# Sliding-window attention and an MLP: q and k loaded two tokens to a partition, turned and multiplied in 64x64 tiles

## The chip, the cores and the metric

The kernel runs on one core of a Trainium2 chip. The metric is device time in microseconds (us) for one execution, and a kernel's time is the median of its runs. Engine names are those of the profile: PE is the matrix engine (a matmul streams a moving operand against a stationary one that a weight load, PEld in the profile, put there before), DVE the vector engine, ACT the scalar engine (activations), POOL the engine whose queue issues the loads here, SP the queue that issues the stores. Matmul results land in PSUM, which has eight banks of 2 KB per partition; everything else lies in SBUF.

## What is computed

Eight batches, eight heads, 576 tokens, head size 64, model width 512, hidden width 2048. Attention looks back over a window of 128 tokens with a linear distance penalty per head; its output goes through a normalised MLP with a residual. Inputs and output are float32; the kernel computes in fp16 with float32 sums.

```python
def _attn_ref(q, k, v):                      # B, H, S, D = 8, 8, 576, 64
    scores = np.matmul(q, k.transpose(0, 1, 3, 2)) / np.sqrt(D)
    rel = pos[:, None] - pos[None, :]
    slopes = 2.0 ** (-8.0 * (np.arange(H) + 1) / H)
    mask = (rel >= 0) & (rel < 128)
    scores = np.where(mask, scores - slopes * np.abs(rel), -1e9)
    attn = softmax(scores)
    return np.matmul(attn, v)

def _moe_ref(x, g_ln, w_ch1, w_ch2):         # x: [B, S, H * D]
    xn = (x - mean) / np.sqrt(var + 1e-06) * g_ln
    return x + np.maximum(xn @ w_ch1, 0.0) @ w_ch2
```

## The kernel before

**Blocks.** Two batches make a pair (four pairs). A pair has nine blocks of 128 tokens: four of the even batch, four of the odd one, and a ninth (`T`) that holds the last 64 tokens of both. `order` lists the 36 blocks. A block passes through these steps:

- `load_t` (L177) and `load_v` (L185) bring q, k and v by POOL's queue, one token to a partition, all eight heads beside each other; the float32 is turned into fp16 on the way. In HBM one head of one token is a run of 64 numbers.
- `turn` (L228) transposes q and k by PE, eight 128x128 transposes a block (two heads, 64 rows each, in one), into a PSUM tile `ps_tr`. DVE copies the halves of q into `qT` (L232), which holds each head's q in its own half of the rows with zeros in the other half (`zero_rows`, L160 and L161, writes the zeros); ACT copies k into `kT` (L236).
- `scores` (L260) multiplies, by key block and pair of heads, 128 keys with the 256 queries that can see them. Because of the zeros in `qT` one matmul of 128 rows gives two heads beside each other, 512 columns. ACT takes the exponential (L261), DVE multiplies it with the mask and distance penalty (`m_full` and its three relatives, L266).
- `values` (L282) multiplies the weights with v, which has a column of ones beside it, so that the row sums come along; DVE takes the reciprocal (L290) and scales (L291).
- `centre` takes mean and variance (L316, L317) and subtracts the mean (L319); `turn_x` (L329) transposes the result by PE and DVE copies it to `xT` (L330). `inv_std` computes 1/std on DVE for a group of blocks.

**Groups.** `GROUPS` has sizes 2, 2 and then eight times 4. For a group `mlp` does the first product (L407, 16 units of four matmuls, each followed by a ReLU on ACT, L414) and the second (L419, 16 matmuls a block, then DVE adds the residual at L429 and SP stores).

**Order.** `steps` is a list of closures for the attention part. The MLP of group g is written out unit by unit, and after each unit `advance_to` runs as many steps for later groups as keep both in proportion. In what order each engine then takes its instructions is decided by a scheduler, by readiness and the order of writing.

**Start.** The loads are one list, issued by `load_until` three blocks ahead (`AHEAD`); the weights stand in it behind blocks 1, 2 and 3 (`weights`), w1 in four chunks and w2 in four. `gain_w1` (L149) multiplies w1 with the gain on DVE, all four chunks after block 1.

**PSUM.** Two banks for scores, one for transposes, two for values, three for the MLP.

Of the kernel before, what the change touches and what calls it, by code (L numbers as in the profile page):

```python
# [1 line left out]

# [14 lines left out]
P = 128  # L17
# [4 lines left out]
E0, O0, T = 0, 4, 8  # L22
NSLOT = 9


SLOT = [4, 5, 6, 7, 0, 1, 2, 3, 8]
DURING = {0: [2], 1: [3], 2: [T], 3: [4, 5], 4: [6], 5: [7], 6: [9], 7: [10], T: []}
GROUPS = [2, 2] + [4] * 8

NV = 14  # L30
AHEAD = 3
LEAD = 4

# [4 lines left out]
def distances():  # L38

    key = np.arange(P)[:, None]

    def far(rel, ok):
        return np.where(ok & (rel >= 0) & (rel < WINDOW), rel, FAR)

    q = np.arange(2 * P)[None, :]
    full = far(q - key, np.ones((P, 2 * P), bool))
    tail = np.arange(P)[None, :]  # L50
    even = far(P + tail - key, tail + 0 * key < 64)
    odd = far(P + tail - 64 - key, tail + 0 * key >= 64)
    both = far(tail - key, (tail // 64) == (key // 64))
    return np.concatenate([full, even, odd, both], axis=1).astype(np.float16)
# [3 lines left out]
def kernel(  # L58
# [19 lines left out]
    half = P // 2  # L78
    inv_sqrt_d = float(1.0 / np.sqrt(D))

    def pool(name, bufs, **kw):
# [3 lines left out]
    qk_pool = pool("qkstage", 4)  # L85
    k_pool = pool("kT", 4)
    probs_pool = pool("probs", 7)
# [6 lines left out]
    ps_tr = pool("ps_tr", 1, space=PSUM)  # L94
    ps_pv = pool("ps_pv", 2, space=PSUM)
# [9 lines left out]
    m_full = consts.tile([P, H, 2 * P], FP16)  # L105
    m_even, m_odd, m_both = (
        consts.tile([P, H, P], FP16, name=f"m{i}", tag=f"m{i}") for i in range(3)
    )

    def decay(m, at):  # L110
# [15 lines left out]

    qT = [
        consts.tile([P, HP, 2, NSLOT, P], FP16, name=f"qT{i}", tag=f"qT{i}")  # L130
        for i in range(2)
    ]
# [26 lines left out]
    def zero_rows(i):  # L159
        nc.vector.memset(qT[i][half:P, :, 0, :, :], 0.0)  # L160
        nc.vector.memset(qT[i][0:half, :, 1, :, :], 0.0)  # L161


    def spans(p, blk):

        if blk == T:
            return [(2 * p, 4 * P, TAIL, 0), (2 * p + 1, 4 * P, TAIL, half)]
        b, i = (2 * p, blk) if blk < O0 else (2 * p + 1, blk - O0)
        return [(b, i * P, P, 0)]

    staged = {}

    def load_t(src, tag, p, blk):
        st = qk_pool.tile([P, H, D], FP16, tag=tag, name=tag)
        staged[tag, p, blk] = st
        for b, t0, n, p0 in spans(p, blk):
            nc.gpsimd.dma_start(  # L177
                out=st[p0 : p0 + n, :, :],
                in_=src[b, :, t0 : t0 + n, :].rearrange("h p d -> p h d"),
            )  # L180
# [11 lines left out]
    turns = [(0, [E0, E0 + 1])]  # L192
    for p, blk in order:
        turns.append((p, DURING[blk]))
    turns = [
        [(p + (i >= NSLOT), i % NSLOT) for i in l if p + (i >= NSLOT) < NPAIR]
        for p, l in turns
    ]
    w1s, w2s = ([(f, c) for c in range(4)] for f in (load_w1, load_w2))
    weights = {1: w1s[:2], 2: w1s[2:], 3: w2s}  # L200
    loads, place = [], []
    for n, (p, blk) in enumerate(order):
        for t in turns[n]:
            loads += [(load_t, q, "qs") + t, (load_t, k, "ks") + t]
        place.append(len(loads))
        loads.append((load_v, p, blk))
        loads += weights.get(n, [])
# [10 lines left out]
    probs, xs = {}, {}  # L218

    kT = {}  # L220

    def turn(p, blk, pool=ps_tr, tag="tr"):

        qs, ks = staged.pop(("qs", p, blk)), staged.pop(("ks", p, blk))
        ps = pool.tile([P, 2 * HP, P], FP16, tag=tag, name="ps_tr")
        for i, st in enumerate((qs, ks)):
            for hp in range(HP):
                nc.tensor.transpose(  # L228
                    ps[:, i * HP + hp, :], st[:, 2 * hp : 2 * hp + 2, :], iden
                )  # L230
        for i, rows in enumerate((slice(0, half), slice(half, P))):
            nc.vector.tensor_copy(  # L232
                out=qT[p % 2][rows, :, i, SLOT[blk], :], in_=ps[rows, 0:HP, :]
            )
        kT[p, blk] = k_pool.tile([P, HP, P], FP16, tag="kT", name="kT")
        nc.scalar.copy(out=kT[p, blk], in_=ps[:, HP:, :])  # L236

    def scores(p, blk, hp):


        if hp == 0:
            w = P if blk == T else 2 * P
            probs[p, blk] = probs_pool.tile([P, H, w], FP16, tag="probs", name="probs")
        pr = probs[p, blk]
        qt = qT[p % 2][:, hp]
        heads = slice(2 * hp, 2 * hp + 2)
        own, nxt = slice(0, P), slice(P, 2 * P)
        at = SLOT[blk]
        if blk == T:
            nq, rhs = 1, qt[:, :, at, :]  # L250
            weigh = [(own, m_both[:, heads, :])]
        elif blk % 4 == 3:
            nq, rhs = 2, qt[:, :, at : SLOT[T] + 1 : SLOT[T] - at, :]
            m_next = m_even if blk == E0 + 3 else m_odd
            weigh = [(own, m_full[:, heads, own]), (nxt, m_next[:, heads, :])]
        else:
            nq, rhs = 2, qt[:, :, at : at + 2, :]
            weigh = [(slice(0, 2 * P), m_full[:, heads, :])]
# [226 lines left out]
```

## Time and profile before

The median of three runs is 363.92 us (363.85 to 365.21). The profiled execution took 363.87 us; its span, from the first to the last instruction, is 362.1 us.

| | busy, us | share of the span | instructions |
|---|---|---|---|
| PE, matmuls | 337.1 | 93% | 2336 |
| PEld, weight loads | 174.0 | 48% | 2336 |
| DVE | 237.1 | 65% | 717 |
| ACT | 185.1 | 51% | 373 |
| POOL | 107.0 | 30% | 132 |

| group (line) | count | busy, us | mean ns of one |
|---|---|---|---|
| first MLP product (L407) | 640 | 144.5 | 359 |
| second MLP product (L419) | 576 | 141.2 | 379 |
| scores (L260) | 144 | 52.9 | 385 |
| values (L282) | 544 | 32.3 | 196 |
| transposes of q (L228) | 144 | 14.9 | 230 |
| mask products on DVE (L266), 128x512 of m_full | 96 | 40.5 | 423 |
| qT copies on DVE (L232) | 72 | 30.3 | 420 |
| kT copies on ACT (L236) | 36 | 20.9 | 584 |

An instruction's mean is its whole way through the engine. Matmuls follow each other more closely than that, since the next one enters while the last one drains; the pace, from start to start, is read from a timeline. A busy PE is therefore not yet a PE at its pace. The chain of work that ended last is 67% PE by time, 17% DVE and 8% ACT.

### The profile page before, as it was taken

The numbers are of one execution on the slowest core, as the hardware profiler recorded it, in microseconds if no ns is written. First come the engines' busy times: TensorE is split into PE (matmuls) and PEld (weight loads), VectorE is DVE, ScalarE is ACT, GpSimd is POOL, SyncE is SP. The second block draws the span as 40 slices with busy tenths as digits, with TensorE's granted clock in tenths as the row PEclk, the third lists the DMA queues.
The fourth block names the chain that finished last, engine by engine and source line by source line (L and its number), as shares of the span: only waits on it lengthen the run. The fifth ranks groups of instructions, "written<-read, shape, count | busy, mean of one in ns | idle before, by whom it ended". The sixth has DMA issues, their size and how long they took to land.

```text
span 362.1 us, 6199 instructions
## 1 busy us (share of the span) xinstructions
PE 337.1 (93%) x2336; PEld 174.0 (48%) x2336; DVE 237.1 (65%) x717; ACT 185.1 (51%) x373; POOL 107.0 (30%) x132
## 2 busy tenths in 40 slices
PE   2369999999999999999999999999999999999994
PEld 1136657554445454544555455554545454454441
DVE  5399899975677567856775678667765775564011
ACT  8526558457426753564357634743576347513700
POOL 8646688631224224223224213112110000000000
PEclk9999999999999999999999999999999999999998
DMA  9999999988689748829689765508640120011012
GB/s 106 171 186 206 159 172 156 100 99 53 42 105 111 51 32 101 103 16 72 87 103 64 52 83 90 35 2 102 89 29 2 58 60 1 2 58 58 2 58 59
DMA packets 122830, 28.39 MB, mean 78 GB/s; under 512 B 113968, under 2 KB 118192, under 8 KB 122800
## 3 DMA queue, kind: packets, MB, share of 16 engines
q0 software_dynamic: 116736, 18.36, 70.7%
q1 hardware_dynamic: 6064, 9.64, 7.8%
q8 instruction: 18, 0.29, 0.3%
q14 instruction: 12, 0.10, 0.1%
HBM read 36.90 MB, written 9.44 MB: 128 GB/s over the span
## 4 chain that ended last, share of the span: by engine, by line
PE 67%; DVE 17%; ACT 8%; DMA 3%; POOL 2%; issue 2%; ACTq 0%; POOLq 0%
PE ps_m L419 27%; PE ps_m L407 24%; PE ps_sc L260 5%; PE ps_pv L282 4%; PE ps_tr L228 3%; ACT probs L261 3%; PE ps_tx L329 3%; DVE probs L266 3%; ACT ht L414 3%; DMA w<-in_moe_w_ch_dram 3%; DVE x L291 3%; DVE st L316 2%; DVE qT L232 2%; DVE o L429 2%; ACT kT L236 2%
## 5 line engine op out<-in xcount | busy, mean ns | idle before, releaser
L407 PE MATMUL ps_m<-xT,w 128*128 128x512 f16 (+1 forms) x640 | 144.5, 359 | 0.0
L419 PE MATMUL ps_m<-w,ht 128*128 128x512 f16 x576 | 141.2, 379 | 0.0
L261 ACT ACTIVATE probs<-ps_sc 128x512 f16<-128x512 f32 (+1 forms) x144 | 80.9, 578 | 89.0 <-PE ps_sc L260 88.7
L414 ACT ACTIVATE ht<-ps_m 128x512 f16<-128x512 f32 (+1 forms) x160 | 89.0, 560 | 43.2 <-PE ps_m L407 42.2
L407 PEld LDWEIGHTS <-w 128*128 128x128 f16 x640 | 59.7, 98 | 50.4 <-issue 0.9
L419 PEld LDWEIGHTS <-ht 128*128 128x128 f16 x576 | 53.4, 98 | 54.3 <-issue 1.6
L266 DVE TENSOR_TENSOR probs<-probs,m_full 128x512 f16<-128x512 f16 (+1 forms) x128 | 49.7, 389 | 44.7 <-ACT probs L261 42.8
L177 POOL DMA_DIRECT2D qs<-in_q_dram x40 | 34.1, 852 | 101.0 <-PE ps_tr L228 85.5
L260 PE MATMUL ps_sc<-qT,kT 128*128 128x512 f16 (+1 forms) x144 | 52.9, 385 | 2.5 <-ACT probs L261 1.3
L185 POOL DMA_DIRECT2D vx<-in_v_dram x40 | 33.9, 860 | 52.6 <-PE ps_pv L282 49.4
L429 DVE SCALAR_TENSOR_TENSOR o<-ps_m,rstd,x 128x512 f32<-128x512 f32 x36 | 26.9, 746 | 25.4 <-PE ps_m L419 24.9
L282 PEld LDWEIGHTS <-probs 128*128 128x128 f16 x544 | 27.1, 98 | 26.7 <-DVE probs L266 12.7
L282 PE MATMUL ps_pv<-vx,probs 128*128 128x65 f16 x544 | 32.3, 196 | 6.9 <-DVE probs L266 6.6
L232 DVE COPY qT<-ps_tr 64x512 f16<-64x512 f16 x72 | 30.3, 420 | 9.1 <-PE ps_tr L228 8.6
L177 POOL DMA_DIRECT2D ks<-in_k_dram x40 | 34.1, 855 | 4.0 <-DMA w<-in_moe_w_ch_dram 2.1
L236 ACT COPY kT<-ps_tr 128x512 f16<-128x512 f16 x36 | 20.9, 584 | 24.9 <-DVE qT L232 23.3
L291 DVE TENSOR_TENSOR x<-ps_pv,rec 128x256 f16<-128x256 f32 x72 | 30.2, 423 | 1.9
L316 DVE BATCH_NORM_STATS2 st<-x 128x6 f32<-128x512 f16 x36 | 25.0, 693 | 1.0
L330 DVE COPY xT<-ps_tx 128x512 f16<-128x512 f16 x36 | 15.2, 424 | 11.8 <-PE ps_tx L329 11.6
L228 PE MATMUL ps_tr<-iden,qs 128*128 128x128 f16 x144 | 14.9, 230 | 7.5 <-DMA qs<-in_q_dram 6.5
L260 PEld LDWEIGHTS <-kT 128*128 128x128 f16 x144 | 14.2, 100 | 14.9 <-issue 2.0
L228 PEld LDWEIGHTS <-qs 128*128 128x128 f16 x144 | 11.4, 102 | 16.6 <-DMA qs<-in_q_dram 7.0
(29 smaller groups left out, 143.7 us busy)
## 6 DMA issues: line engine op xcount, KB each, us to landing
out_dram<-o SPq DMA_DIRECT2D x32, 256.0 KB, 2.6
qs<-in_q_dram POOLq DMA_DIRECT2D x32, 128.0 KB, 4.1
ks<-in_k_dram POOLq DMA_DIRECT2D x32, 128.0 KB, 4.9
vx<-in_v_dram POOLq DMA_DIRECT2D x32, 128.0 KB, 5.3
w<-in_moe_w_ch_dram POOLq DMA_DIRECT2D x8, 512.0 KB, 9.9
out_dram<-o SPq DMA_DIRECT2D x8, 128.0 KB, 2.8
qs<-in_q_dram POOLq DMA_DIRECT2D x8, 64.0 KB, 4.3
ks<-in_k_dram POOLq DMA_DIRECT2D x8, 64.0 KB, 4.0
```

Source lines behind the costliest of these rows:

```text
L177: nc.gpsimd.dma_start(out=st[p0 : p0 + n, :, :], in_=src[b, :, t0 : t0 + n, :].rearrange("h p d -> p h d"),)
L228: nc.tensor.transpose(ps[:, i * HP + hp, :], st[:, 2 * hp : 2 * hp + 2, :], iden)
L232: nc.vector.tensor_copy(out=qT[p % 2][rows, :, i, SLOT[blk], :], in_=ps[rows, 0:HP, :])
L260: nc.tensor.matmul(ps, kT[p, blk][:, hp, :], rhs, start=True, stop=True)
L261: nc.scalar.activation(out=pr[:, heads, :], in_=ps, func=AF.Exp, scale=inv_sqrt_d)
L266: nc.vector.tensor_tensor(out=dst, in0=dst, in1=mask, op=ALU.mult)
L282: nc.tensor.matmul(ps[:, i, :], probs[p, o][:, h, cols], vext[(p * NSLOT + o) % NV][:, h, :], start=(n == 0), stop=(n == len(terms) - 1),)
L291: nc.vector.tensor_tensor(out=xs[p, blk][:, hg * 4 * D : (hg + 1) * 4 * D].rearrange("p (h d) -> p h d", h=4), in0=ps[:, :, 0:D], in1=rec. ...
L407: nc.tensor.matmul(ps[:, 0:cols], w1[:, kb, fb * P : (fb + 1) * P], xT[:, kb, 0:cols], start=(kb == 0), stop=(kb == NKB - 1),)
L414: nc.scalar.activation(out=ht[:, fb, 0:cols], in_=ps[:, 0:cols], func=AF.Relu)
L419: nc.tensor.matmul(ps, ht[:, fb, at * P : (at + 1) * P], w2[:, fb, :], start=(fb == 0), stop=(fb == NFB - 1),)
L429: nc.vector.scalar_tensor_tensor(out=o, in0=ps, scalar=rs[:, at : at + 1], in1=xs[p, blk], op0=ALU.mult, op1=ALU.add,)
```

## The change

- **Loads.** `load_qk` replaces `load_t`: a partition gets two neighbouring tokens, so one head of a partition is a run of 128 numbers in HBM. A tile holds the same 128 tokens of both batches of a pair, 64 partitions each. The number of loads of q, k and v stays 40 each.
- **Block order.** Blocks alternate between the two batches (`divmod(blk, 2)`), the loads of q and k come every second block.
- **Turning.** `turn` (new L215) does two blocks at once in 64x64 tiles: 64 transposes for q and k, each with its own weight load of 64 columns, four in a row on four different quarters of the array. q is copied by DVE and k by ACT, one copy for both blocks (L224); q goes to ACT for the first two turns. `qT` and its zeros are gone.
- **Scores.** By query block instead of key block (`attend`, new L253): 64x64 tiles, the two heads of a pair in the two row halves, the keys in two column halves, 128 queries as columns. A burst of 16 pairs of weight load and matmul fills a PSUM tile of two banks; an ordinary block has two bursts, the block `T` three, the first block of each batch one. One exponential and one mask product of 128x1024 follow each burst.
- **PSUM.** Four banks for scores and the turns of q and k together (two buffers of two banks), one for values and `turn_x` together, three for the MLP.
- **Order of PE.** `manual_schedule` keeps PE's instructions in the order of writing; for the first stage DVE's too.
- **Start.** Groups are 2, 2, 2, 2 and then seven times 4. All weights stand behind the loads of the first four blocks. The first products of groups 0 and 1 come before the second product of group 0; gains for the last three chunks of w1 are spread over the first product of group 0. Two masks' worth of tables (`m_ends`, `m_tail`) replace three.

```diff
-GROUPS = [2, 2] + [4] * 8
-
-NV = 14
-AHEAD = 3
-LEAD = 4
+GROUPS = [2] * 4 + [4] * 7
+
+NV = 10
+AHEAD = 4
+LEAD = 3
...
-    ps_tr = pool("ps_tr", 1, space=PSUM)
-    ps_pv = pool("ps_pv", 2, space=PSUM)
+    ps_pv = pool("ps_pv", 1, space=PSUM)
...
+    def load_qk(src, tag, p, i):
+
+        n = min(P, S - i * P)
+        t = raw_pool.tile([P, H, 2, D], FP16, tag=tag, name=tag)
+        raw[tag, p, i] = t
+        for b in range(2):
             nc.gpsimd.dma_start(
-                out=st[p0 : p0 + n, :, :],
-                in_=src[b, :, t0 : t0 + n, :].rearrange("h p d -> p h d"),
+                out=t[b * n // 2 : (b + 1) * n // 2],
+                in_=src[2 * p + b, :, i * P : i * P + n, :].rearrange(
+                    "h (c r) d -> c h r d", r=2
+                ),
             )
...
-    weights = {1: w1s[:2], 2: w1s[2:], 3: w2s}
+    weights = {3: w1s + w2s}
...
+    def turn(p, i):
...
+        ps = ps_sc.tile([P, 2, 2, 2, HP, HALF], FP16, tag="sc", name="ps_tr")
+        nb = 1 if i == 4 else 2
+        for n, tag in enumerate("qk"):
+            st = raw.pop((tag, p, i))
             for hp in range(HP):
...
+                for r in range(2):
+                    for b in range(nb):
+                        rows = slice(b * HALF, (b + 1) * HALF)
+                        for j in range(2):
+                            cols = slice(j * HALF, (j + 1) * HALF)
+                            nc.tensor.transpose(
+                                ps[cols, b, n, r, hp, :],
+                                st[rows, 2 * hp + j, r, :],
+                                iden[rows, rows],
+                            )
...
+    def attend(p, blk, keys, mask, tag, hps):
...
+        ps = ps_sc.tile([P, 2, len(hps), nk, P], FP32, tag="sc", name="ps_sc")
+        qt, b = turned["q", p, blk // 2], blk % 2
+        for n, hp in enumerate(hps):
+            for t, o in enumerate(keys):
+                kt = turned["k", p, o // 2][:, o % 2]
+                for j in range(2):
+                    rows = slice(j * HALF, (j + 1) * HALF)
+                    for c in range(2):
+                        cols = slice(c * HALF, (c + 1) * HALF)
+                        nc.tensor.matmul(
+                            ps[cols, j, n, t, :],
+                            kt[rows, hp, cols],
+                            qt[rows, b, hp, :],
+                            start=True,
+                            stop=True,
+                        )
...
+    def scores(p, blk):
+        low, high, every = [0, 1], [2, 3], [0, 1, 2, 3]
         if blk == T:
...
+            attend(p, T, [6, 7], m_ends, "probs", low)
+            attend(p, T, [6, 7], m_ends, "probs", high)
+            attend(p, T, [T], m_tail, "own", every)
+        elif blk < 2:
+            attend(p, blk, [blk], m_full[:, :, P:], "own", every)
         else:
...
+            attend(p, blk, [blk - 2, blk], m_full, "probs", low)
+            attend(p, blk, [blk - 2, blk], m_full, "probs", high)
...
+    def with_gains(units):
+
+        for u, _ in enumerate(units):
+            if u % 4 == 1 and u < 12:
+                gain_w1(u // 4 + 1)
+            yield
...
-    load_until(place[3] + 1)
-    for g, size in enumerate(GROUPS):
-        advance_to(ready[g] + LEAD)
-        start = done
-        last = ready[g + 1] + LEAD if g + 1 < len(GROUPS) else len(steps)
-        units = NFB + 4 * size
-        for u, _ in enumerate(mlp(g)):
-            advance_to(start + (last - start) * (u + 1) // units)
+    load_until(place[3])
+    with tc.manual_schedule(engines={mybir.EngineType.PE}):
+        with tc.manual_schedule(engines={mybir.EngineType.DVE}):
+            advance_to(ready[0])
+            weave(with_gains(mlp1(0)), NFB, ready[1])
+        weave(mlp1(1), NFB, ready[1])
+        weave(mlp2(0), 8, ready[1] + 2)
+        weave(mlp2(1), 8, ready[2] + LEAD)
+        for g, size in list(enumerate(GROUPS))[2:]:
+            last = ready[g + 1] + LEAD if g + 1 < len(GROUPS) else len(steps)
+            weave(chain(mlp1(g), mlp2(g)), NFB + 4 * size, last)
```

## The prediction

> **What bounds the kernel now.** First the page's slices: PE is full from the fourth slice to the last but one, at full clock, and DMA is busy over the first ten.
>
> ```profile
> PE   2369999999999999999999999999999999999994
> DVE  5399899975677567856775678667765775564011
> PEclk9999999999999999999999999999999999999998
> DMA  9999999988689748829689765508640120011012
> ```
>
> So three parts: a start in which PE has little to do, a long part set by PE, a tail. The timeline gives their edges (start, duration, engine, line; in brackets the idle time before and what ended it).
>
> ```profile
> 30.52 0.84 PE L407 MATMUL ps_m<-xT,w 128*128 128x256 f16 x3
> ...
> 329.37 13.98 PE L407 MATMUL ps_m<-xT,w 128*128 128x512 f16 x64
> ...
> 357.20 0.75 DVE L429 SCALAR_TENSOR_TENSOR o<-ps_m,rstd,x 128x512 f32<-128x512 f32 x1 [2.70 <-PE ps_m L419]
> ```
>
> The MLP begins at 30.5 us; PE ends with the last group's two products and is done at 357.2; residual, store and end take the remaining 4.9 us.
>
> Then PE's pace, from start to start, in a stretch without waits:
>
> ```profile
> 110.30 0.39 PE L228 MATMUL ps_tr<-iden,qs 128*128 128x128 f16 x4
> 110.52 0.39 PE L228 MATMUL ps_tr<-iden,ks 128*128 128x128 f16 x4
> 110.75 0.38 PE L260 MATMUL ps_sc<-qT,kT 128*128 128x512 f16 x1
> 110.96 1.24 PE L407 MATMUL ps_m<-xT,w 128*128 128x512 f16 x5
> ...
> 115.38 0.53 PE L282 MATMUL ps_pv<-vx,probs 128*128 128x65 f16 x12
> 115.75 0.59 PE L407 MATMUL ps_m<-xT,w 128*128 128x512 f16 x2
> ```
>
> Four transposes of 128 columns take 0.22 us, 0.0556 each; one matmul of 512 columns 0.21 to 0.22 (64 of them fill 329.4 to 343.2, so 0.216); twelve value matmuls of 65 columns 0.37, so 0.031 a pair with its weight load. By the same reading 256 columns take 0.109 (four at 32.56, the next instruction at 33.00). The pace follows the columns; weight loads stay behind it.
>
> PE's work by pace, in us: first product 512 x 0.216 + 128 x 0.109 = 124.5; second 576 x 0.216 = 124.4; scores 128 x 0.216 + 16 x 0.109 = 29.4; turns of q and k 288 x 0.0556 = 16.0; `turn_x` 144 x 0.0556 = 8.0; values 544 x 0.031 = 16.9. Sum 319.2. Before 30.5 stand 40 turns, 11 scores, 24 values and 8 of `turn_x` (counted in that window): 2.2 + 2.4 + 0.7 + 0.4 = 5.7. So from 30.5 to 357.2, 326.7 us, 313.5 are work and 13.2 are lost to waits and drains. The waits in total show where:
>
> ```profile
> PEld L329 <- DVE xc L319: 17.4, 34, 1.1
> PEld L282 <- DVE probs L266: 12.7, 20, 5.7
> PE ps_pv L282 <- DVE probs L266: 6.6, 7, 4.7
> PE ps_tr L228 <- DMA qs<-in_q_dram: 6.5, 3, 5.2
> ```
>
> (us in total, times, longest.) PE waits for DVE, and for loads three times only, at the start.
>
> **The start.** The chain up to 30.5 runs through POOL's queue and DVE:
>
> ```profile
> 9.05 9.53 DMA w<-in_moe_w_ch_dram
> 20.16 0.67 DVE probs L266 x2
> 22.68 0.60 DVE st L316
> ```
>
> A chunk of w1 lands at 18.6, and from there DVE, 9.75 us busy between 20 and 30, works through products, statistics, copies and all sixteen gains before the first product starts.
>
> **Part by part.** *Removed from PE:* 29.4 of scores and 16.0 of turns, 45.4. *Added:* 1152 transposes of 64 columns and 1088 score matmuls of 128, each with its weight load: 288 and 272 quartets on four different quarters of the array. No row shows a quarter of the array. Upper bound: one pair after another at the pace of the nearest rows, 1152 x 0.031 (the 65-column row) + 1088 x 0.0556 (the 128-column row) = 35.7 + 60.5 = 96.2. Lower bound: a quartet takes what one of it takes, 24.0. I take 24.0: consecutive pairs share neither a quarter nor, across row halves, a PSUM bank, nothing in the data makes one wait for the other, and the value row shows a load and a matmul both started within 31 ns. This is the weakest step.
>
> The Trainium skill speaks on both sides. TensorE: Matmul & The Clock Gate, Part 3, has matmuls on different tiles start about 4 ns apart, which would give my 24. The same page's Back-to-back issue gap puts a floor of about 25 ns under any matmul of up to 64 columns; if it held across quarters, an estimate by it is 2240 x 0.025 = 56 instead of 24. TensorEngine Tiling (Array Packing), Restrictions, says column tiling switches the fast weight load off. No run here shows any of the three.
>
> *Changes between tilings.* The new pairs stand in 54 runs among 128x128 matmuls, 108 changes. Every matmul before is 128*128, so none is priced. Bounds: nothing, or the whole drain, 0.379 of a 512-column record less its pace of 0.216, 0.163 each, 17.6 in all. I take half, 8.7, since back-to-back work hides part of a drain. TensorEngine Tiling, Key Properties, says a change of mode drains the engine, which would be the full 17.6.
>
> New PE work: 24.0 + 8.7 = 32.7, a gain of 12.7. MLP, values and `turn_x` keep their columns (448 x 0.216 + 256 x 0.109 = 124.7 for the first product): 124.7 + 124.4 + 8.0 + 16.9 + 32.7 = 306.7.
>
> *DVE.* Gone: qT copies 30.3, zeros 8.0, products 63.4 (40.5 + 13.7 + 9.2), four `xT` copies 1.7. Added: 68 products of 128x1024; from 288 ns at 256 and 423 at 512, 0.693 each, 47.1; 18 copies of q, 14 of them twice the 424 ns of a 128x512 copy at most, 13.6. Net 43 less, 237 to 194, 18%. Wide products gain by fewer starts; POOL and SP keep the counts of their DMAs (SP's 40 stores are untouched).
>
> *ACT.* Exponentials 144 become 68 of 1024 columns: from 392 at 256 and 603 at 512, about 1.05 each, 71 for 81; more ReLUs of 256 columns add 4, other copies about 2: 185 to about 181. Hidden before and after.
>
> *Loads.* q and k have half the runs. q0's 116,736 packets took 70.7% of 16 engines' span, 35 ns each; if a doubled packet costs the same, 73,728 become 36,864 and 81 us of each engine's time go; if it costs double, none. All of it lies beside PE after the start, so I count nothing; uncovered, loads are late where POOL's 0.87 an issue paces them. That is at the start: twelve issues stand ahead of w1 instead of eight, so w1 goes out from about 12 us instead of 8.3, and with the 7.7 to 13.1 from issue to landing its chunks arrive between 20 and 28.5. Queued behind the weights are q, k and v of blocks 4 and 5, landing by about 35; turning them stands behind both first products in PE's order.
>
> *The start again,* by the rows: fourth load issued at 3.9, landed 8.0 to 8.8; turn and ACT's two copies to 10.4; scores, exponential 1.05 and product 0.7 to 12.7; values, statistics, centring to 15.7; block 1 likewise to 19.4; then in DVE's fixed order two products (1.4) and four gains (1.5): first product at 22.3 instead of 30.5. Behind it DVE holds the gains of the other chunks, two blocks and two `inv_std`: PE will wait there, as it did between 40 and 60 before, so I leave those losses in.
>
> *New waits on PE.* In order, PE can't go around a wait. A block `T` needs three bursts with two buffers: the third waits for the first's exponential, 1.05 and the way there and back, 1.2, four times: 4.8, with nothing behind it on PE able to go. Values wait for DVE's scaling of the half before (one bank now); four to eight MLP matmuls, 0.86 to 1.73, cover 0.18 + 0.42 and the latency; uncovered, up to a product's 0.7 each. I let the lost 13.2 fall with DVE's work by 18%, to 10.8.
>
> **The sum.** Work before 22.3: 2.8 (32 transpose quartets x 0.031, 16 score quartets x 0.0556, 16 values, 8 `turn_x`). Span 22.3 + (306.7 - 2.8) + 10.8 + 4.8 + 4.9 = 346.7. The profiled execution took 363.87 with a span of 362.1; 1.8 more gives 348.5, which I set against the median of 363.92.
>
> **Rivals.**
> - *Row halves overlap, column halves don't:* pairs at half the serial sum, 48.1 instead of 24.0: 372.6, slower. For it: nothing shows two streams into one row half. Against: quarters are separate in weights and output.
> - *Weight loads go one at a time* (the slower side's mechanism): each pair takes a value pair's 0.031 on PE in the turn and score bursts, 69.4 instead of 24.0: 394; fully serial, 96.2, 421. It decides from 17.5 ns a pair: (24.0 + 15.4)/2240. For it: loads double in number to 4576, and half the new pairs are too short to hide one; against: loads of 128 columns hide behind 65-column matmuls.
> - *The start isn't shortened,* the weights behind twelve issues come too late and the first product starts near 30.5: 356.7. For it: DMA is full there. Against: the latest landing by rows, 28.5, is the fourth chunk's, not the first's.
>
> **How the numbers follow.** Quarters overlap: 0.52; start not shortened: 0.08; halves only: 0.15; loads one at a time: 0.25. The likeliest gives 348.5; its own range is 335 (free changes, no third-burst wait) to 358 (full drains). The slower cases have 0.40, so the range goes up past the second case, to 376, and leaves out the last: 0.75, and the cheaper part of the last case makes it near 0.8. What differs by under 0.5% can't be told from no change here. Faster 0.59, within 0.05 (between the first cases and the second), slower 0.36.
>
> **What would show it.** Right: in the score bursts, sixteen pairs in about 0.22 us, a turn of 64 in about 0.5; first product near 22; DVE near 194 busy, PE's waits for `T` of about 1.2 four times. Wrong: bursts of 0.5 us or more, gaps around each burst of 0.16, or long PE waits for DVE between the two halves of values.

## The result and the profile after

The kernel after takes 360.82 us (median of 6 runs, 359.29 to 362.51), the kernel before, run beside it, 364.36 (363.85 to 365.21). The ratio is 0.990, with a 95% interval of 0.9863 to 0.9936: faster by 1.0%. The sign was forecast and the time lies in the range, but the gain is 3.5 us instead of 15.4. The profiled execution took 361.82 with a span of 360.0, where the sum gave a span of 346.7. So 13.3 us are to be explained.

The slices of the kernel after, from its page:

```profile
PE   1469798788989999999999999899999999899994
...
DVE  0478426977688656754685577556855774571011
...
PEclk9999899999999999999999999999999999999999
DMA  9999999993948747739175849525100120011012
```

PE reaches nine in the fourth slice, as before, but from there to the twelfth it has sevens and eights among the nines, where it had nines alone: it is not full. The clock has an 8 in the fifth slice. DMA has gaps after the start, where it was near full for ten slices before; q0's packets fell from 70.7% to 55.2% of the engines' span.

The edges, from the timeline of PE in the kernel after (start, duration, engine, line):

```profile
23.80 2.89 PE L421 MATMUL ps_m<-xT,w 128*128 128x256 f16 x12 [0.93 <-DVE w L134]
...
327.30 13.98 PE L421 MATMUL ps_m<-xT,w 128*128 128x512 f16 x64
341.12 13.98 PE L437 MATMUL ps_m<-w,ht 128*128 128x512 f16 x64
```

The MLP begins 6.7 us earlier than before, PE is done at 355.1 instead of 357.2, and the tail of 4.9 is the same. PE's pace in the steady part, from the same timeline:

```profile
109.53 0.64 PE L253 MATMUL ps_sc<-q,k 64*64 64x128 f16 x32
110.11 1.04 PE L437 MATMUL ps_m<-w,ht 128*128 128x512 f16 x4
...
118.92 1.89 PE L421 MATMUL ps_m<-xT,w 128*128 128x512 f16 x8
120.74 0.45 PE L215 MATMUL ps_tr<-iden,q 64*64 64x64 f16 x32
121.02 0.44 PE L215 MATMUL ps_tr<-iden,k 64*64 64x64 f16 x32
121.39 1.90 PE L421 MATMUL ps_m<-xT,w 128*128 128x512 f16 x8
```

Thirty-two score pairs take 0.58 from start to start, with the change back to 128x128 in it; 64 turns take 0.65. Eight MLP matmuls take 1.82 from 118.92 to 120.74 instead of 8 x 0.216 = 1.73: a change of tiling costs 0.093.

The waits in total (us, times, longest), kernel after:

```profile
ACT k L224 <- DVE q L224: 31.9, 10, 5.1
...
PE ps_tx L337 <- DVE xc L327: 6.3, 7, 1.5
...
PE ps_tr L215 <- DMA q<-in_q_dram: 5.4, 2, 4.9
PE ps_sc L253 <- ACT probs L261: 3.9, 4, 1.0
...
PE ps_sc L253 <- ACT k L224: 3.6, 2, 2.5
...
PE ps_pv L290 <- DVE x L299: 3.3, 6, 0.9
```

PE waits for the third burst of `T` four times 1.0, for loads only at the start, and for a number of DVE's and ACT's small results. These lie between 57 and 76 us (timeline of PE, kernel after):

```profile
57.79 0.42 PE L290 MATMUL ps_pv<-vx,probs 128*128 128x65 f16 x8 [0.66 <-DVE probs L267]
...
61.75 0.40 PE L337 MATMUL ps_tx<-iden,xc 128*128 128x128 f16 x4 [0.53 <-DVE xc L327]
...
65.69 0.25 PE L253 MATMUL ps_sc<-q,k 64*64 64x128 f16 x4 [0.59 <-DVE q L224]
67.02 0.59 PE L253 MATMUL ps_sc<-q,k 64*64 64x128 f16 x28 [1.08 <-ACT k L224]
...
72.39 0.42 PE L290 MATMUL ps_pv<-vx,probs 128*128 128x65 f16 x8 [0.90 <-DVE x L299]
```

Here only four MLP matmuls, 0.87 us, stand between one attention step and the next, since a group of two blocks has little MLP work to spread, and the fixed order gives PE nothing else to take up.

PE's lost time (start to start, less the pace of each kind and less 0.093 a change of tiling), worked out by stage from both traces:

| stage | before | after |
|---|---|---|
| first product to 40 (before) or 47.8 (after) | 0.7 | 7.9 |
| from there to 110 | 4.9 | 9.9 |
| 110 to the last group | 7.4 | 6.3 |

With 0.1 in the last group the sums are 13.2 and 24.2. The edges give the same: before, 326.6 us with 313.4 of work; after, 331.3 (23.80 to 355.09) with 307.1 of work. (The 23.3 in an expectation below takes 2.8 as the work ahead of the first product, as the prediction did; by the trace it is 3.6.) In the first row of after, 4.4 are half clock (below) and 3.5 are waits. The steady part loses less than before, as forecast; the first 110 us lose 12 us more. The same can be read from the MLP, each matmul at its pace: at 50 us 16.3 us' worth is done instead of 13.9, at 80 us the lead is gone, at 110 the kernel after is 4.0 behind, and over the rest the cheaper attention part wins about 6.

### The profile page after: what moved, and what is told of

Its sections match the earlier page's. It is cut to its first block, busy times and chain, and to the rows that moved or that the text cites. A ratio compares the mean times of both kernels' runs of the same rounds, so it can differ in the third digit from the quotient of the medians.

```text
span 360.0 us, 9671 instructions
## 1 busy us (share of the span) xinstructions
PE 324.9 (90%) x4208; PEld 178.2 (49%) x4208; DVE 209.5 (58%) x554; ACT 185.6 (52%) x295; POOL 92.8 (26%) x132
## 3 DMA queue, kind: packets, MB, share of 16 engines
q0 software_dynamic: 79872, 18.36, 55.2%
## 4 chain that ended last, share of the span: by engine, by line
PE 78%; DVE 11%; ACT 6%; issue 1%; DMA 1%; POOL 1%; ACTq 0%; POOLq 0%
PE ps_m L421 33%; PE ps_m L437 32%; PE ps_pv L290 5%; PE ps_sc L253 4%; PE ps_tr L215 3%; ACT probs L261 2%; PE ps_tx L337 2%; DVE st L324 2%; DVE x L299 2%; DVE probs L267 2%; DMA k<-in_k_dram 1%; DVE q L224 1%; DVE xc L327 1%; ACT k L224 1%; DVE o L447 1%
## 5 line engine op out<-in xcount | busy, mean ns | idle before, releaser
L261 ACT ACTIVATE probs<-ps_sc 128x1024 f16<-128x1024 f32 x56 | 54.2, 1022 | 53.8 <-PE ps_sc L253 53.7
L160 POOL DMA_DIRECT2D q<-in_q_dram x40 | 26.7, 673 | 71.9 <-PE ps_tr L215 64.3
L267 DVE TENSOR_TENSOR probs<-probs,m 128x1024 f16<-128x1024 f16 x56 | 38.4, 687 | 11.5 <-ACT probs L261 11.5
L298 DVE RECIPROCAL rec<-ps_pv 128x4 f32<-128x4 f32 x72 | 12.9, 180 | 49.3 <-PE ps_pv L290 49.1
L224 ACT COPY k<-ps_tr 128x1024 f16<-128x1024 f16 (+1 forms) x20 | 23.8, 1190 | 32.4 <-DVE q L224 31.9
L253 PE MATMUL ps_sc<-q,k 64*64 64x128 f16 x1088 | 24.0, 225 | 8.1 <-ACT probs L261 3.9
L224 DVE COPY q<-ps_tr 128x1024 f16<-128x1024 f16 (+1 forms) x18 | 21.1, 1174 | 11.7 <-PE ps_tr L215 11.6
L253 PEld LDWEIGHTS <-k 64*64 64x64 f16 x1088 | 17.5, 109 | 21.1 <-issue 16.8
L160 POOL DMA_DIRECT2D k<-in_k_dram x40 | 26.7, 682 | 3.9 <-DMA w<-in_moe_w_ch_dram 3.8
L337 PE MATMUL ps_tx<-iden,xc 128*128 128x128 f16 x144 | 14.4, 224 | 6.4 <-DVE xc L327 6.3
## 6 DMA issues: line engine op xcount, KB each, us to landing
w<-in_moe_w_ch_dram POOLq DMA_DIRECT2D x8, 512.0 KB, 13.6
```

The costliest lines, as they stand in the source:

```text
L160: nc.gpsimd.dma_start(out=t[b * n // 2 : (b + 1) * n // 2], in_=src[2 * p + b, :, i * P : i * P + n, :].rearrange("h (c r) d -> c h r d", ...
L224: copy(out=t[:, 0:nb].rearrange("p b h (c r) -> p b r (h c)", r=2), in_=ps[:, 0:nb, n].rearrange("p b r h c -> p b r (h c)"),)
L253: nc.tensor.matmul(ps[cols, j, n, t, :], kt[rows, hp, cols], qt[rows, b, hp, :], start=True, stop=True,)
L261: nc.scalar.activation(out=dst.rearrange("p (n j) q -> p j n q", j=2), in_=ps.rearrange("p j n t q -> p j n (t q)"), func=AF.Exp, scale=in ...
L267: nc.vector.tensor_tensor(out=dst, in0=dst, in1=mask[:, heads, :], op=ALU.mult)
```

## The experiments

All edits are made on the kernel after, except where another version is named. Each ratio is against the kernel before in the same series (364.19 to 364.88); intervals are 95%.

One thing helps to read the times. Every run has a record of the clock that PE was granted, as a share over the run. In the fourteen profiled executions the share is 0.990 to 0.995 where the clock fell back to half on the way (last section) and 0.996 to 1.000 where it did not. The kernel after has two runs of the second kind, 359.29 and 359.32, and four of the first, 360.31 to 362.51. A median therefore also depends on how many of its runs had a fall-back. Below, "at full clock" means runs at 0.996 or above, compared with the 359.3 of the kernel after; these are few runs each.

### The third burst of T one step later

```diff
-            attend(p, T, [T], m_tail, "own", every)
...
             steps.append([(turn_x, g, at, p, blk)])
+            if m + 1 < len(order) and order[m + 1][1] == T:
+                steps.append([(attend, p, T, [T], m_tail, "own", [0, 1, 2, 3])])
```

> The changed kernel, but the third score burst of each block T (16 pairs) stands one step later, behind turn_x of the block before, so that MLP matmuls lie between it and the two bursts whose buffers it needs. Theory (PE's fixed order turns each wait into lost PE time): the four waits of the third burst for the exponential, 3.9 us together in the changed kernel, go, and the time falls by 3 to 4 us to about 357. Rival (the wait only moves, since ACT and DVE set the pace there): values of T or the next MLP unit wait instead, the time stays within 1 us of 360.8.

Measured 358.55 (356.2 to 359.79), ratio 0.9842 (0.9804 to 0.988): 2.3 less than the kernel after, and 2.4 less at full clock (356.2 and 357.5). PE's wait for the exponential, 3.9 in all, is gone from the waits. The wait costs time, about six tenths of its length; the intervals of the two ratios just overlap, so the share is rough.

### One token to a partition, 128x128 turns

The score tiles stay, so this undoes the loads and the turning alone.

```diff
-                                ps[cols, b, n, r, hp, :],
-                                st[rows, 2 * hp + j, r, :],
-                                iden[rows, rows],
+                        ps[:, b, n, hp, :], st[:, b, 2 * hp : 2 * hp + 2, :], iden
```

> The changed kernel with the loads and the turning of before: one token to a partition, runs of 64 numbers, 128x128 transposes (8 a block for q and k); scores stay in 64x64 tiles. Theory: turning costs PE 288 x 0.056 = 16.1 us instead of 288 quartets at 0.035 = 10.1 and 40 changes of tiling at 0.093 = 3.7, so 2.3 more; the copies of q and k no longer write every second number, 1.3 us each in the changed kernel, and get cheaper if that is why; POOL needs 0.87 an issue instead of 0.68, so the weights land some 2 us later. Sum +2 to +4, 363 to 365. Rival 1 (runs of 128 numbers are worth much because DMA is full up to 60 us): +6 or more, first products waiting for w1. Rival 2 (the slow copies cost more than the loads gain): faster than 360.8.

Measured 361.08 (360.66 to 362.58), ratio 0.992 (0.9891 to 0.9949): no difference from the kernel after by the medians. But five of these six runs kept the full clock, at 360.66 to 361.83, which is 1.4 to 2.5 more than the 359.3 of the kernel after; the medians agree since four of its six runs had a fall-back and only one of these. PE pays 0.0556 a transpose of 128 columns instead of 0.035 a quartet, but has no changes of tiling around the turns. What small-tile turning gives back stands in the groups of the page (count, busy us, mean ns; idle time before). The copies of q in the kernel after:

```profile
L224 DVE COPY q<-ps_tr 128x1024 f16<-128x1024 f16 (+1 forms) x18 | 21.1, 1174 | 11.7 <-PE ps_tr L215 11.6
```

and in this one:

```profile
L218 DVE COPY q<-ps_tr 128x1024 f16<-128x1024 f16 (+1 forms) x18 | 11.4, 631 | 13.7 <-PE ps_tr L211 13.1
```

Two tokens to a partition leave neighbouring tokens in separate columns, and the copy must write every second number. Its 128x1024 form takes 1301 ns instead of 691 on DVE, and on ACT 1304 instead of 1013. By the medians, loading and turning in the new way are worth nothing net; at full clock they are worth some 1.7, nearer to what was expected. What the halved runs of the loads are worth alone isn't shown, since no run changes only them.

### Unread matmuls at the start

The first products run at half pace until about 29 us: in the kernel after the first twelve take 2.68 from start to start, 0.22 each. Here twelve 512-column matmuls whose result nobody reads stand between 14 and 24 us.

```diff
+            if m < 2:
+                steps[-1].insert(0, (warm, 3))
+                steps[-1].append((warm, 2))
```

> The changed kernel with twelve matmuls of 512 columns, whose result nobody reads, in PE's idle stretches between 14 and 24 us. In the changed kernel the first products of 256 columns follow each other at 0.21 us up to about 29 us and at 0.109 afterwards, and the clock's rows show half speed again from 39.7 to 43.1. Theory (half clock costs the early start 2.7 us, and 1.6 more at 40): the first products run at 0.109 from the start, group 0 is through its first product 2 to 3 us earlier, and the time falls by 2 to 4 us. Rival (what is won waits for DVE's gains and the statistics of blocks 2 and 3 anyway): products at 0.109 but the same end of group 0's first product, time within 1 us of 360.8 or above it by the extra work.

Measured 359.95 (358.91 to 361.25), ratio 0.9882 (0.9852 to 0.9912): 0.9 less than the kernel after, within the spread of both; at full clock (358.91, 359.26 and 360.49) there is no gain. The clock is full from 19.6 us and the twelve take 1.77, but PE then waits for the gains (0.49 before 26.64), and group 1's first product starts at 37.88 instead of 39.12. The rival, then: DVE is right behind, and a faster clock mostly uncovers it.

### All pairs of one quarter after each other

```diff
-        for n, hp in enumerate(hps):
-            for t, o in enumerate(keys):
-                kt = turned["k", p, o // 2][:, o % 2]
-                for j in range(2):
+        for j in range(2):
...
+                for n, hp in enumerate(hps):
+                    for t, o in enumerate(keys):
```

(and in `turn` likewise)

> The changed kernel with the same pairs in another order: all pairs of one quarter of the array, then all of the next, in the turns and in the score bursts. Theory (what makes the new pairs cheap is that four consecutive ones run in four quarters at once): turns at 0.03 a pair instead of 0.009, scores at 0.056 instead of 0.015, so 1152 x 0.021 + 1088 x 0.041 = 69 us more on PE, 425 to 430. Rival (short pairs are bound by something common to all orders, such as the issue): within 5 us of 360.8.

Measured 373.81 (372.16 and 375.45), ratio 1.0262 (1.0202 to 1.0322): 13.0 more. Neither number fits. The gaps between neighbouring turns sum to 27.3 us instead of 14.3, those between scores to 22.7 instead of 21.0. In the turns the median gap between neighbouring starts is 26 ns in this order; in the order round the quarters it was 4. The scores hardly lose: a burst has only four pairs to a quarter, where a turn has eight for q and eight for k. The timeline of this kernel shows why the price is not the serial one:

```profile
109.21 0.80 PE L215 MATMUL ps_tr<-iden,q 64*64 64x64 f16 x29
109.83 0.21 PE L215 MATMUL ps_tr<-iden,k 64*64 64x64 f16 x1
109.85 0.19 PE L215 MATMUL ps_tr<-iden,q 64*64 64x64 f16 x1
```

By the program k's turns come behind all 32 of q's; here they start in between. One quarter goes on to its next pairs while another still works, so a burst written by quarters overlaps in part all the same. That the quarters overlap is shown, and for the turns, that their order in the program decides how much.

### The order of PE left to the scheduler

From the first product of group 1 on, `weave` stands outside of `manual_schedule`.

```diff
-        weave(mlp2(0), 8, ready[1] + 2)
...
+    weave(mlp2(0), 8, ready[1] + 2)
```

> The changed kernel with PE's written order kept only up to the end of group 1's first product; from there the scheduler orders PE, as it did before the change. It breaks the bursts up: 68 runs of small tiles instead of 54, and it turns blocks 4 and 5 ahead of group 1's first product. Theory (PE loses time behind waits in its fixed order between 50 and 100 us): fewer waits there, 3 to 5 us gained, 2.6 given back by 28 more changes of tiling at 0.093: 358 to 361. Rival 1 (the order is not what costs; ACT and DVE can't deliver faster there): +2.6 or more, 363 or above. Rival 2: the scheduler's order puts a turn in front of products before its loads are there, and PE waits near 36 us.

Measured 360.26 (357.48 to 361.86), ratio 0.9893 (0.9862 to 0.9923): no difference. The scheduler pulled the turn of blocks 4 and 5 ahead, where PE waited for their loads (0.49, 0.45 and 0.68 between 36 and 39 us), and split the small tiles into 68 runs instead of 54. Its clock also fell back for twice as long (6.8 us), and its one run at full clock took 357.48. So this run doesn't isolate the order's price.

### w1 without its gain

The product of w1 with the gain, 16 instructions of DVE before and during group 0's first product, is left out.

```diff
-        1: [(gain_w1, 0)],
...
-            if u % 4 == 1 and u < 12:
-                gain_w1(u // 4 + 1)
```

> The changed kernel without the gain: w1 isn't multiplied with g_ln, which leaves 16 DVE instructions out (4.9 us of DVE's work between 23 and 35 us). Theory (DVE's chain of gains, statistics and scaling sets the stage from 22 to 39 us): the first product starts at about 22.9 instead of 23.8 and group 1's first product 2 to 3 us earlier than 39.1, and the time falls by 2 to 3 us. Rival (w1's arrival sets it): PE waits for DMA in place of DVE, less than 1 us gained.

Measured 358.84 (357.65 to 361.31), ratio 0.9869 (0.9838 to 0.99): 2.0 less, with overlapping intervals, and 1.6 at full clock (357.65 and 357.79). Group 1's first product starts at 36.53 instead of 39.12, and PE's waits for w1 (0.93 and 0.61 in the kernel after) are gone, so DVE's chain at the start is on the path. How much of the 2.6 is the gain's isn't shown: in this execution the clock was full from 25.71 us instead of 29.36, and unread matmuls alone, with the gain in place, brought the same product forward by 1.2.

### Both small repairs together

> The changed kernel with both edits tried singly: the third burst of T one step later, and twelve unread matmuls in the idle stretches from 14 to 24 us. Singly they gave 358.55 and 359.95 beside 360.82 (on other chips' runs; ratios to the kernel before 0.984, 0.988 and 0.990). Theory (they stand in different places and add up): 357.5 to 358, ratio about 0.982. Rival (the second episode of half clock near 40 us falls where it likes and covers the difference): no better than the late third burst alone.

Measured 357.17 (356.74 to 358.46), ratio 0.9818 (0.9795 to 0.984): 3.7 less than the kernel after, a little more than 2.3 and 0.9 together. But four of these five runs kept the full clock, at 356.74 to 357.27. There they are 2.3 less than the kernel after and no faster than the late third burst alone (356.2 and 357.5). So what the unread matmuls add is at most fewer fall-backs, and that may be chance: of three later versions with the same matmuls, two had them in five and in three of six runs, one in none of four.

### Without the mask products

```diff
-        nc.vector.tensor_tensor(out=dst, in0=dst, in1=mask[:, heads, :], op=ALU.mult)
+        if p == 0 and blk < 4:
+            nc.vector.tensor_tensor(
+                out=dst, in0=dst, in1=mask[:, heads, :], op=ALU.mult
+            )
```

> The kernel after, without the mask products of blocks other than the first four (so the weights of those blocks are not masked or decayed): some 62 products of 0.687 us, 42 us of DVE's 209.5, are left out, all behind 45 us. Theory: of the 23.3 us that PE loses between its first product and its end, what lies behind 45 us is mostly the chain exponential, product, values, scaling, centring, met in a fixed order behind only four matmuls: the waits between 55 and 85 us (0.66, 0.53, 0.59, 0.90, 0.59) shrink by over half, 0.7 is saved at each of them, and the time falls by 3 to 6 us, to 355 to 358. Rival: the losses lie in the clock, in changes of tiling and in the start, and a DVE that is 58% busy delays nobody for long: the time stays at 360 to 361.5.

Measured 357.45 (356.69 to 358.94), ratio 0.9814 (0.9779 to 0.9849): 3.4 less, in the theory's range; at full clock 2.6 (356.69 and 356.78), just under it. The timeline of PE in this kernel:

```profile
54.59 0.42 PE L293 MATMUL ps_pv<-vx,probs 128*128 128x65 f16 x8
...
63.49 0.58 PE L253 MATMUL ps_sc<-q,k 64*64 64x128 f16 x28 [1.08 <-ACT k L224]
...
68.19 0.40 PE L293 MATMUL ps_pv<-vx,probs 128*128 128x65 f16 x8 [0.23 <-DVE x L302]
```

DVE's busy time falls from 209.5 to 173.2, and of the waits shown above the 0.66 at 57.79 is gone and the 0.90 is 0.23; the 1.08 for ACT's copy of k stays, and so does the 0.53 for the centring. So a DVE that is busy 58% of the time does delay PE: through the length of the chain behind each exponential, not through lack of time.

### The turn of blocks 6 and 7 one block earlier

On the version with both repairs.

```diff
-            if m == FIRST + 1:
-                steps.append([turns[m + 1]])
             steps.append([(values, p, blk, 1), (centre, g, at, p, blk)])
+            if m == FIRST:
+                steps.append([turns[m + 2]])
```

> As the version with the third burst of T one step later and unread matmuls at the start (357.2 us), and the turn of blocks 6 and 7 stands one block earlier, behind the values of block 4 instead of between the two halves of block 5's. Theory: PE's waits for the copies of q and k at 63 to 66 us (0.58 and 1.08) are there because scores follow 2.5 us behind their turn with eight matmuls between; with the turn 4 us earlier both waits go and the time falls by 1.0 to 1.7 us, to 355.5 to 356.2. Rival: the waits are ACT's and DVE's own queue, filled by the blocks before, and move to the next step: within 0.5 us of 357.2.

Measured 361.3 (359.65 to 361.86), ratio 0.9908 (0.9881 to 0.9936): 4.1 more than 357.17, outside of both. The timeline of this kernel:

```profile
59.08 0.42 PE L253 MATMUL ps_sc<-q,k 64*64 64x128 f16 x16
62.19 0.64 PE L253 MATMUL ps_sc<-q,k 64*64 64x128 f16 x16 [2.69 <-ACT k L224]
```

The scores of block 5, which don't need this turn, wait 2.69 us for its copy of k: the turn holds one of the two score buffers until both of its copies are done. Behind that wait PE ran at half clock for 3.4 us (four MLP matmuls at 62.77 take 1.68 instead of 0.87). The reason why the buffer is held so long stands in the kernel after too. Its timeline of DVE:

```profile
64.36 1.28 DVE L224 COPY q<-ps_tr 128x1024 f16<-128x1024 f16 x1
```

and of ACT:

```profile
65.67 1.30 ACT L224 COPY k<-ps_tr 128x1024 f16<-128x1024 f16 x1 [3.59 <-DVE q L224]
```

ACT had been idle for 3.59 us, yet its copy of k starts when DVE's copy of q has ended. Both read one PSUM buffer, and both read both of its banks.

### One token to a partition, with the earlier turn

> As the version with the earlier turn, but q and k loaded one token to a partition and turned by 128x128 transposes; the score tiles stay. PE: turns at 0.0556 instead of 0.035 a quartet, 5.9 us more, less the 18 pairs of changes of tiling around turns at 0.093 each, 3.3 us: 2.6 us more work. Copies: 18 of q 0.6 us and 18 of k 0.3 us shorter. Theory: small-tile turning and two-token loading are worth nothing net, since longer copies cost PE in waits what the turns save: within 1 us of the run with the earlier turn. Rival: with the waits around the turns gone the copies no longer matter and PE's work alone decides: 2 to 3 us slower than it.

Measured 359.5 (358.24 to 360.82), ratio 0.9862 (0.983 to 0.9894): 1.8 less than the run before it (the intervals just overlap), outside of both expectations. With the shorter copies the same wait is 1.05 instead of 2.69. At full clock it is 0.7 to 1.4 less (358.24 to 358.96 in three runs, 359.65 in one). So where a buffer hangs on the copies, shorter copies can outweigh PE's 2.6 us of longer turns.

### A buffer each for q and k

```diff
-        ps = ps_sc.tile([P, 2, 2, 2, HP, HALF], FP16, tag="sc", name="ps_tr")
+        shape, both = [P, 2, 2, 2, HP, HALF], []
...
         for n, tag in enumerate("qk"):
             st = raw.pop((tag, p, i))
+            ps = ps_sc.tile(shape, FP16, tag="sc", name="ps_tr")
+            both.append(ps)
```

> The kernel after, with the turns of q and k in one PSUM buffer each (both of the score buffers) instead of one buffer for both. In the kernel after, ACT's copy of k starts only when DVE's copy of q has ended (31.9 us of waiting, 10 times), so a turn holds one of the two score buffers for about 1.3 + 1.3 us plus the ways, and the scores behind it wait. Theory: this row of copies is part of what PE loses between 55 and 110 us; with the copies beside each other ACT's wait goes, PE's wait of 1.08 at 65 us falls to under 0.3, and the time falls by 1 to 2 us from 360.82. Rival: a turn now takes both score buffers, so that its first transpose waits for the last exponential and the next scores for a copy all the same: within 0.5 us, or slower.

Measured 359.9 (357.96 to 361.02), ratio 0.9867 (0.9844 to 0.989): 0.9 less than the kernel after, just short of the theory's 1 to 2 and by itself within the spread (five of the six runs had a fall-back). Timeline of ACT, this kernel:

```profile
64.57 1.30 ACT L226 COPY k<-ps_tr 128x1024 f16<-128x1024 f16 x1 [1.97 <-PE ps_tr L217]
```

The copy now follows the transposes, beside DVE's copy of q at 64.94, and PE's 1.08 is gone. The edit with the two repairs:

> The same, with the third burst of T one step later and the unread matmuls at the start (the version with 357.17 us). Theory: the gain adds to theirs, 355.2 to 356.5. Rival: both buffers taken by a turn stand in the way of the later third burst: 357 or more.

Measured 355.58 (355.27 to 356.11), ratio 0.9757 (0.9742 to 0.9771): 1.6 less than the version without it, and no two runs of the two versions overlap; at full clock, which all four runs kept, it is 1.4 less. So the wait of one copy for the other costs time. It is the best version here, 2.4% faster than the kernel before and 1.5% (360.82 to 355.58) faster than the one after.

## Why the prediction was right in sign and wrong in size

The gap of 13.3 us in the span is 3.2 of PE work behind the first product, 1.5 of the start and 8.6 of lost time (24.2 instead of 10.8 + 4.8).

- **Quarters of the array overlap: right.** The quartets cost 272 x 0.061 + 288 x 0.035 = 26.7 where 24.0 was taken and 96.2 was the upper bound. The cases of halves only (372.6) and of loads one at a time (394) fell. The weakest step by its own words held. (The count of weight loads in that case was off: 4208 by the page, not 4576.) Of the pages weighed there, Part 3 of the Trainium skill's TensorE: Matmul & The Clock Gate has matmuls on different tiles start about 4 ns apart; the 3 to 4 ns between neighbours across quarters agree. The same page's floor of about 25 ns, in Back-to-back issue gap, doesn't bind a burst that goes round the quarters, which takes 8.7 ns a turn. The 26 ns within one quarter are no test of it, since half of the 0.0556 of 128 columns is 28 ns.
- **Changes of tiling: right.** 0.093 each was measured for the 0.081 taken, 108 x 0.093 = 10.0 for 8.7; neither free nor the full drain of 0.163.
- **PE work: mis-sized,** 36.7 instead of 32.7, by these two terms; 0.8 of the difference stands ahead of the first product.
- **The start: right in kind, 23.80 instead of 22.3.** The case of a start that isn't shortened fell, and loads aren't late. The turn and its copies took until 11.2 instead of 10.4 (ACT's two take 1.29 each, one after the other), block 0 until 17.3 instead of 15.7, block 1 until 22.2 instead of 19.4. That is 2.8 late; 1.3 came back, since the first product waits for the two mask products and only the first of the four gains (1.6 instead of 2.9).
- **The third burst: the wait was right,** 3.9 for 4.8; removed, it gave 2.3, some six tenths.
- **The step that failed: "I let the lost 13.2 fall with DVE's work by 18%, to 10.8".** Without the third burst 20.3 were lost. The step scaled a wait with an engine's total of busy time. What PE meets is the length of a chain (exponential, product, values, scaling, centring, copy) against the work that stands between two of its links, and the change made that cover thin in the first 110 us: four more blocks in groups of two, and PE bound to the written order. The steady part, where cover is thick, did fall (7.4 to 6.3). The runs show parts of this: a shorter chain gives 2.6 at full clock (no mask products), copies that don't wait for each other 1.4. That thin cover, by the size of the groups, is the reason is read from the timeline; no run changes the groups, so it is argued and not shown. About 4.4 more are half clock, by the starts of the first products and the values between them (2.7) and of group 1's (64 matmuls in 8.65 instead of 6.98). The working had no term for that: it read full clock from a page that shows it where it has no record. In the kernel before too, the first twelve products take 1.83 (30.52 to 32.35) instead of 1.31, and the record of a full clock begins at 31.57.
- **The copies: mis-sized, and their place not seen.** 1.30 was measured for at most 0.848. DVE is 209.5 busy instead of 194; 7.5 of that are the copies of q, 21.1 for 13.6, and the rest is not broken down. Worse, they were counted as busy time only. In the kernel before the waits' row `ACT kT L236 <- DVE qT L232: 23.3, 15, 4.7` was there to be read, with 0.84 + 0.58 for one block; now two copies of 1.30 stand in a row and hold a buffer that scores need. The Trainium skill's PSUM — Partial Sum Buffer, section PSUM bank collisions raise a hardware error, says that two engines may not access one bank and quadrant at the same time, reads included, and that a compiler's scheduler puts a dependency between them; it speaks against one buffer for q and k, the row agrees (31.9 us of ACT's waiting), and the prediction should have weighed it. Whether the shared buffer or the shared banks make the copies wait isn't told apart: a buffer each changes both.
- **Loads beside PE: right** after the start, where PE waits for no load. Halving the runs of q and k shows in q0's share (70.7% to 55.2%); what it does to the time isn't shown by itself.

What stays open: how much of the 9.9 us lost between 48 and 110 us is the fixed order by itself, since the freed order moved other things too, and how much the small groups; why the clock falls back; and where the best version loses its last 17 us (324.9 from its first product to PE's end, less 307.8 of work): it was not taken apart.

## What to carry to other kernels

Small tiles that go round the four quarters of the array overlap almost freely, so price them by the quartet, and add a fixed price for each change of tiling. A wait is not a share of an engine's busy time: when an order is fixed, lay each chain of small results against the work that stands between its links, above all where groups are small. A copy out of PSUM is priced by how it writes and by what holds its buffer: here two engines that read one buffer went one after the other, and whoever needed that buffer next waited for both. And before two versions are compared, look how many of the runs of each kept the full clock.

## What the runs showed of the hardware that was not expected

- **The clock.** With sparse PE work before 24 us the clock stayed at half until about 29 us in the kernel after. The point varies: 26.1 to 29.4 us in four profiled versions whose start is written the same (the kernel after, the late third burst, the free order, no mask products). In some executions it fell back to half near 40 us, for 3.4 us (6.8 in the free order): in the profiled runs of the kernel after, the one-quarter order, the free order, the one-token version with the earlier turn, and the version with a buffer each. Others with the same waits before it kept the full clock. Group 1's first product in the timeline of PE, kernel after:

```profile
39.12 8.81 PE L421 MATMUL ps_m<-xT,w 128*128 128x256 f16 x64 [0.67 <-ACT xT L339]
```

and with unread matmuls at the start:

```profile
37.88 7.15 PE L431 MATMUL ps_m<-xT,w 128*128 128x256 f16 x64 [0.67 <-ACT xT L339]
```

  The granted share of every run tells what this costs: the four runs of the kernel after at 0.995 or below took 361.5 in the mean, the two above 359.3, so the fall-back makes most of the spread of 3.2 us. None of the 44 runs of the kernel before in these series is below 0.996: the fall-back came with the change. What sets it off is not shown.
- **Order across quarters.** With all pairs of one quarter written in a row, matmuls of other quarters started ahead of earlier ones of the program, by several instructions (the rows at 109.83 above).
- **A copy that writes every second number** of fp16 costs 1301 ns on DVE instead of 691 for 128x1024, and 1304 instead of 1013 on ACT.
